# Two feed-forward blocks behind attention: when the second block's sixteen first weights are converted

## The chip, the cores and the metric

One core of a Trainium2 chip runs the kernel. The metric is the device time of one execution in microseconds; 1041.17 us is the median of three runs of the kernel before (1039.12 to 1044.33). The engines are called PE (TensorE, the matrix engine), DVE (VectorE), ACT (ScalarE), POOL (GpSimd) and SP, which here only issues DMAs.

## The reference

Attention with a decay is followed by two feed-forward blocks over 2304 tokens of 512 numbers. The first has two first weights (gate and value, 512 x 1536 each) and normalises its input, the second has one (512 x 2048). The weights of both blocks come as 64-bit floats; q, k, v and f are 32-bit.

```python
def _moe_ref(x, w_gate, w_val, w_out, rms_g) -> np.ndarray:
    rms = np.sqrt(np.mean(x * x, axis=-1, keepdims=True) + 1e-06)
    xn = x / rms * rms_g
    g = xn @ w_gate
    silu = g * (1.0 / (1.0 + np.exp(-g)))
    val = xn @ w_val
    return (silu * val @ w_out).astype(np.float32)

def _moe2_ref(x, w_in, w_out) -> np.ndarray:
    h = x @ w_in
    g = h * (1.0 / (1.0 + np.exp(-h)))
    return (g @ w_out).astype(np.float32)
```

## The kernel before

The tokens are cut into two parts, 1280 and 1024 (`PHASES`). After attention (up to about 218 us) the kernel runs `layer` four times: first block "a" for part 0 and part 1, then second block "b" for part 0 and part 1. In the trace these are about 218 to 457, 457 to 647, 647 to 862 and 862 to 1039 us. A layer goes over the hidden columns in groups of two units of 128 columns: six groups in block "a", eight in block "b". Each product is made of three matmuls of high and low parts (`hi` and `lo`, in the trace wh and wl, hh and hl), so that 32-bit numbers keep their precision. Part 0 of block "a" multiplies plainly; the other three layers use the seven products of Strassen's scheme, whose weight sums POOL forms.

A group's work in the program is: the first weights (`unit_plain` or `unit_in`), the two second weights (`unit_out`), then what is done ahead (`unit_ahead`), then the products and, between them, the second products of the group before (`pending`). The weights of a group are so placed by `spread` that their ACT instructions come after the first or the second Silu of the group before; in the trace they run a group ahead of their use.

`weights` brings one unit of 128 columns. If it is not yet kept, SP loads 512 KB of 64-bit numbers into a staging tile `st` (two buffers), ACT takes the upper word's magnitude (L143), and DVE makes the 32-bit float of it in four operations (L144 to L147); then SP stores it as a tile of 256 KB in DRAM (`kept`, L149). If it is kept already, SP loads these 256 KB (L134) and nothing is converted. `unit_ahead` does only the conversion and the store: it takes a tile `f` (three buffers) and makes no high and low parts. After `weights`, `unit_in` forms four sums of each pair on POOL (L162), ACT copies the high parts (L165), DVE or POOL takes the low parts (L166). `unit_plain` has L183 on ACT and L184 on POOL, `unit_out` has L193 on ACT and L194 on POOL. Its tile for the converted numbers has the tag `c` (nine buffers), which the hidden values use too.

In the groups that belong to `EARLY` (the third and the fourth) POOL forms differences of the next part's tokens (L657) and SP stores them (L660). ACT's L738 copies a sum of products out of PSUM while the accumulator goes on; the next product into it waits for that copy. L836 is the Silu and L843 the gate's product with the value.

The order of each engine's instructions is laid out when the program is compiled, by a scheduler that follows program order, priorities and free buffers; on the chip each engine keeps to that order and waits for what it needs.

Of the kernel before, what the change touches and what calls it, by code (L numbers as in the profile page):

```python
# [54 lines left out]

AHEAD_OF = ((0, 1), (2, 3), (12, 13), (14, 15), (), ())


@with_exitstack
def block_kernel(ctx: ExitStack, tc: tile.TileContext, q, k, v, f, w_gate, w_val, w_o1, rms_g, w_in, w_o2, ident_d, sel_d, hot_d, out):
# [572 lines left out]
    def end_attention():  # L635

        finish()
        ending.close()
        banks.update(LATER)
        psum["s"] = psum["x"] = ctx.enter_context(tc.tile_pool(name="psum3", bufs=2, space=PSUM, side="right", reuse_waits="tile"))  # L640
        x2 = ctx.enter_context(tc.tile_pool(name="x2", bufs=1, side="right", reuse_waits="tile"))
        xs.update({nm: [x2.tile([P, 2, TT], F32R, name=nm + p) for p in "hl"] for nm in ("t2", "t1", "t3")})

    def split(hi, lo, src):
        nc.scalar.activation(out=hi, in_=src, func=AF.Copy)  # L645
        nc.vector.tensor_tensor(out=lo, in0=src, in1=hi.bitcast(F32), op=ALU.subtract)  # L646
# [3 lines left out]
    def differences(ph, c):  # L650

        x = xparts[ph]
        made[:] = [ph]
        (b11, b12), (b21, b22) = ([x[:, 2 * i + c, j * TT : (j + 1) * TT] for j in range(2)] for i in range(2))
        t1, t2, t4 = (tmp.tile([P, TT], F32, tag="c", name="c") for _ in range(3))
        for nm, o, u, v in (("t1", t1, b12, b11), ("t2", t2, b22, t1), ("t4", t4, b21, t2), ("t3", b12, b22, b12)):
            nc.gpsimd.tensor_tensor(out=o, in0=u, in1=v, op=ALU.subtract)  # L657
            if nm != "t3":
                d = dram.tile([P, TT], F32, name=f"{nm}_{ph}_{c}_{len(kept)}")
                nc.sync.dma_start(out=d, in_=o)  # L660
                stored.setdefault((ph, nm), []).append(d)

    def prepare(ph, ahead=False):

        x, t = xparts[ph], {}
        b = {(i, j): [x[:, 2 * i + c, j * TT : (j + 1) * TT] for c in range(2)] for i in range(2) for j in range(2)}

        def diff(nm, u, v, to=None):
            if (ph, nm) in stored:
                t[nm] = to or [tmp.tile([P, TT], F32, tag="c", name="c") for _ in range(2)]  # L670
                for o, s in zip(t[nm], stored.pop((ph, nm))):
                    nc.scalar.dma_start(out=o, in_=s)
                return
            t[nm] = to or [tmp.tile([P, TT], F32, tag="c", name="c") for _ in range(2)]
            for o, u_, v_ in zip(t[nm], u, v):
                nc.gpsimd.tensor_tensor(out=o, in0=u_, in1=v_, op=ALU.subtract)

        def parts_(nm, src):
            for c in range(2):
                split(xs[nm][0][:, c], xs[nm][1][:, c], src[c])  # L680

        def p6():
            diff("t1", b[0, 1], b[0, 0], None if ahead else b[0, 0])
            diff("t2", b[1, 1], t["t1"])
            parts_("t2", t["t2"])

        def p7():
            if ph in made:
                t["t3"] = b[0, 1]
            else:  # L690
                diff("t3", b[1, 1], b[0, 1], b[0, 1])
            parts_("t3", t["t3"])

        def p4():
            diff("t4", b[1, 0], t["t2"], b[1, 0])
            parts_("t4", t["t4"])

        def rest():
            if ph == 0:
                for c in range(0, NCC, 2):  # L700
                    split(xs["rest"][0][:, c : c + 2], xs["rest"][1][:, c : c + 2], x[:, c : c + 2, 2 * TT :])

        return dict(
            p1=lambda: parts_("b11", b[0, 0]), p2=lambda: parts_("b21", b[1, 0]), p6=p6, p5=lambda: parts_("t1", t["t1"]), p7=p7, p4=p4, p3=lambda: parts_("b22", b[1, 1]), rest=rest
        )

    def spread(fn, *args):

        i = min(len(places), len(LEAD) - 1)
        places.append(0)  # L710
        if done == [1] and i < 2:

            after = exps[min(SECOND + STRIDE * i, len(exps) - 1)]
        elif marks:
            after = marks[min(LEAD[i], len(marks) - 1)]
        else:
            after = exps[min(PLACE + STRIDE * i, len(exps) - 1)]
        with tc.issue_after(after):
            return fn(*args)
# [96 lines left out]
    def layer(n, w_ins, w_out, second, ph, plain=False, ahead=()):  # L816
        NF = w_out.shape[0] // P
        in_fours[:] = [] if len(w_ins) == 2 and not plain else [True]
        G = 2
        for g in range(0, NF, G):  # L820
            win = [spread(*((unit_plain, w, f"{n}{z}", g) if plain else (unit_in, w, f"{n}{z}", g, ph == 0))) for z, w in enumerate(w_ins)]
            wout = [spread(unit_out, w_out, f"{n}o", m) for m in range(g, g + G)]
            for fn in ahead[g // G] if ahead else ():
                spread(fn)
            places.clear()
            marks.clear()
            done[0] += 1

            coming = prepare(parts_left.pop(0), plain) if g + G >= NF and parts_left else {}
            hs, gates = {}, {}  # L830

            def out_(z, at_, a, w):
                psum_ = plain or at_ == (1, 0) or at_[1] == 2
                if z == 0:
                    hf = tmp.tile([P, TT], F32, tag="c", name="c")[:, :w] if psum_ else a
                    act = nc.scalar.activation(out=hf, in_=a, func=AF.Silu)  # L836
                    marks.append(act.ins)
                    if len(w_ins) == 2:
                        gates[at_] = hf
                        return  # L840
                else:
                    hf = gates[at_]
                    (nc.vector if psum_ or at_ == (0, 1) else nc.gpsimd).tensor_tensor(out=hf, in0=a, in1=hf, op=ALU.mult)  # L843
                few = dict(tag="r", bufs=2) if w < TT else dict(tag="h", bufs=5)
                hh, hl = (hp_.tile([P, w], F32R, tag=few["tag"] + p, name="h" + p, bufs=few["bufs"]) for p in "hl")
                split(hh, hl, hf)
                hs[at_] = hh, hl

            todo, pending[:] = list(pending), []
            order = group(win, out_, ph == 0, plain)  # L850

            if plain and coming:

                for nm in ("p6", "p5", "p7"):
                    coming.pop(nm)()
                coming = dict(tile0=[coming[nm] for nm in ("p1", "p2")], tile1=[coming[nm] for nm in ("p4", "p3")])
                coming = {nm: _p(lambda fns: [fn() for fn in fns], fns) for nm, fns in coming.items()}
            for nm, ps in order:
                for p in ps:
                    p()  # L860
                for fn in todo[: 2 if len(ps) == 2 else 1 + (len(todo) > 7)]:
                    fn()
                    todo.remove(fn)
                coming.pop(nm, int)()
                if not plain and parts_left and nm == "p5" and g // G in EARLY:
                    differences(parts_left[0], EARLY.index(g // G))
            for fn in coming.values():
                fn()
            for fn in todo:
                fn()  # L870
            if plain and g == 0:
                end_attention()
            for j, w in enumerate((TT, TT, CUT - 2 * TT)[: 3 if ph == 0 else 2]):
                pending.extend(second(j * TT, w, lambda i, j=j, hs=hs: hs[i, j], wout, g == 0, g + G >= NF, ph))
# [40 lines left out]
    for c in range(0, NCC, 2):  # L915
        split(xs["rest"][0][:, c : c + 2], xs["rest"][1][:, c : c + 2], xparts[0][:, c : c + 2, 2 * TT :])
    for ph in range(2):
        layer("a", [w_gate, w_val], w_o1, second1, ph, ph == 0, [[_p(unit_ahead, w_in, "b0", m) for m in ms] for ms in AHEAD_OF] if ph else ())
    for ph in range(2):
        layer("b", [w_in], w_o2, second2, ph)  # L920
    for fn in pending:
# [41 lines left out]
```

## Time and profile before

| what | value |
|---|---|
| median of three runs | 1041.17 us (1039.12 to 1044.33) |
| the profiled execution | 1040.62 us |
| its span | 1038.8 us |
| PE busy | 1015.4 us (98%) |
| DVE busy | 759.6 us (73%) |
| ACT busy | 565.1 us (54%) |
| POOL busy | 407.4 us (39%) |
| granted PE clock | 0.998 of full |

The profile is of one execution. Times in it are counted from the span's start. A row of the timeline gives the start, the duration, the engine (with a q for its queue when it issues a DMA), the line of the kernel, the operation, the tiles it writes and reads, and its form; in square brackets stand the idle time of the engine before it and what ended that. Matmuls are pipelined: one begins before the one ahead of it ends.

### The profile page before, as it was taken

The page shows a single profiled execution, that of the slowest core. Times are in us where ns is not written, and L with a number is a line of the kernel's source. Part 1 is how long each engine was busy: PE and PEld are TensorE (multiplying, and loading weights), DVE is VectorE, ACT ScalarE, POOL GpSimd, SP SyncE. Part 2 cuts the span into 40 slices and gives each one's busy share as a digit, 9 for nine tenths or more (in the row PEclk, how much of TensorE's full clock was granted, in tenths as well). Part 3 has the DMA queues.
Part 4 walks back from the last instruction along what each step waited for, and adds up shares of the span by engine and source line. Part 5 has one row for each costly group of instructions (what it writes and reads, how often), then busy time and mean ns, then how long its engine had stood idle before and what let it go on. Part 6 is the DMA issues. An engine that isn't in the chain of part 4 may idle for free.

```text
span 1038.8 us, 16025 instructions
## 1 busy us (share of the span) xinstructions
PE 1015.4 (98%) x5459; PEld 843.5 (81%) x5459; DVE 759.6 (73%) x1509; ACT 565.1 (54%) x1191; POOL 407.4 (39%) x601
## 2 busy tenths in 40 slices
PE   8998999999999999999999999999999999999998
PEld 7877778778888888888887787887787888888886
DVE  7889887877576777976487767968876696366664
ACT  6998989874442323445544446564444465544441
POOL 8776666501121206423355544225533323222300
PEclk9999999999999999999999999999999999999999
DMA  5674443123331524231233221134442234121102
GB/s 140 172 196 108 123 95 101 25 69 115 122 123 68 175 71 143 88 95 61 92 126 128 82 77 55 67 117 152 152 153 82 82 122 142 41 67 56 51 0 82
DMA packets 113009, 104.30 MB, mean 100 GB/s; under 512 B 62768, under 2 KB 83664, under 8 KB 112928
## 3 DMA queue, kind: packets, MB, share of 16 engines
q1 hardware_dynamic: 111200, 100.14, 31.4%
q10 hardware_dynamic: 1728, 3.15, 1.0%
q8 instruction: 43, 0.70, 0.3%
q14 instruction: 38, 0.31, 0.1%
HBM read 77.49 MB, written 25.76 MB: 99 GB/s over the span
## 4 chain that ended last, share of the span: by engine, by line
PE 62%; DVE 8%; issue 3%; POOL 3%; ACT 2%; DMA 1%; POOLq 0%; SPq 0%; ACTq 0%; DVEq 0%
PE t L726 32%; PE s L726 16%; PE x L726 12%; POOL f L162 2%; DVE hl L646 1%; DVE xa L903 1%; DVE wl L166 1%; DVE c L743 1%; DVE c L147 1%; DVE f L146 1%; ACT wh L165 1%; POOL c L843 1%; DMA st<-in_moe_w_in_dram 0%; DMA f<-kepta 0%; POOL wol L194 0%
## 5 line engine op out<-in xcount | busy, mean ns | idle before, releaser
L194 POOL TENSOR_TENSOR wol<-c,woh 128x512 fp32r<-128x512 f32 x54 | 77.0, 1433 | 282.1 <-ACT woh L193 254.6
L646 DVE TENSOR_TENSOR hl<-c,hh 128x512 fp32r<-128x512 f32 (+1 forms) x140 | 111.5, 803 | 51.0 <-ACT hh L645 50.7
L162 POOL TENSOR_TENSOR f<-f 128x256 f32<-128x256 f32 x112 | 89.0, 815 | 132.6 <-DMA f<-keptb 55.3
L645 ACT ACTIVATE hh<-c 128x512 fp32r<-128x512 f32 (+1 forms) x140 | 79.4, 583 | 61.6 <-DVE c L843 26.0
L435 POOL TENSOR_SCALAR dt<-ncb,c8t 128x64 f32<-128x64 f32 (+2 forms) x144 | 78.4, 546 | 38.1 <-DVE nm L451 31.5
L738 ACT ACTIVATE c<-t 128x512 f32<-128x512 f32 x84 | 49.5, 590 | 71.7 <-PE t L726 69.1
L463 ACT ACTIVATE pr<-pr,nm 128x192 f32<-128x192 f32 (+3 forms) x144 | 80.2, 558 | 13.4 <-DVE nm L451 10.9
L836 ACT ACTIVATE c<-c 128x512 f32<-128x512 f32 x66 | 41.6, 630 | 80.3 <-DVE c L743 80.3
L166 DVE TENSOR_TENSOR wl<-f,wh 128x1024 fp32r<-128x1024 f32 (+1 forms) x48 | 61.0, 1279 | 31.3 <-ACT wh L165 31.3
L451 DVE CUSTOM_DVE_ANT_0 pr<-s,dt 128x256 f32<-128x256 f32 (+7 forms) x160 | 69.9, 451 | 16.8 <-PE t L472 5.1
L165 ACT ACTIVATE wh<-f 128x1024 fp32r<-128x1024 f32 (+1 forms) x56 | 54.1, 975 | 39.5 <-POOL f L162 19.7
L472 PE MATMUL t<-ident,pr 128*128 128x128 f32 x384 | 69.1, 279 | 3.2 <-ACT pr L463 2.3
L184 POOL TENSOR_TENSOR wl<-f,wh 128x1024 fp32r<-128x1024 f32 x12 | 28.7, 2391 | 93.9 <-ACT wh L183 93.9
L726 PE MATMUL s<-hh,woh 128*128 128x512 f32 (+1 forms) x172 | 64.2, 374 | 0.3 <-DVE xa L885 0.3
L726 PE MATMUL s<-hl,woh 128*128 128x512 f32 (+1 forms) x172 | 64.0, 372 | 0.0
L726 PE MATMUL s<-hh,wol 128*128 128x512 f32 (+1 forms) x172 | 64.0, 372 | 0.0
L743 DVE TENSOR_TENSOR c<-t,c 128x512 f32<-128x512 f32 x60 | 41.2, 687 | 30.2 <-ACT c L738 16.5
L836 ACT ACTIVATE c<-t 128x512 f32<-128x512 f32 (+1 forms) x74 | 37.5, 511 | 41.8 <-PE t L726 40.1
L903 DVE TENSOR_TENSOR xa<-x,xa 128x512 f32<-128x512 f32 x64 | 43.6, 681 | 21.0 <-PE x L726 20.9
L726 PE MATMUL x<-wol,hh 128*128 128x512 f32 (+1 forms) x146 | 57.1, 391 | 1.8 <-POOL wol L194 1.8
L885 DVE TENSOR_TENSOR xa<-s,xa 128x512 f32<-128x512 f32 (+1 forms) x72 | 45.6, 639 | 16.3 <-PE s L726 16.3
L726 PE MATMUL x<-woh,hh 128*128 128x512 f32 (+1 forms) x146 | 56.8, 389 | 0.0
(234 smaller groups left out, 3191.1 us busy)
## 6 DMA issues: line engine op xcount, KB each, us to landing
st<-in_moe_w_out_dram SPq DMA_DIRECT2D x28, 512.0 KB, 3.7
st<-in_moe_w_in_dram SPq DMA_DIRECT2D x16, 512.0 KB, 3.9
st<-in_moe_w_gate_dram SPq DMA_DIRECT2D x12, 512.0 KB, 4.0
kepta<-f SPq DMA_DIRECT2D x24, 256.0 KB, 2.4
st<-in_moe_w_val_dram SPq DMA_DIRECT2D x12, 512.0 KB, 4.6
f<-kepta SPq DMA_DIRECT2D x24, 256.0 KB, 2.6
f<-keptb SPq DMA_DIRECT2D x24, 256.0 KB, 2.6
out_dram<-xa SPq DMA_DIRECT2D x17, 256.0 KB, 2.0
```

Of the source, the lines that this page charges most:

```text
L162: nc.gpsimd.tensor_tensor(out=out_, in0=x, in1=y, op=op)
L165: nc.scalar.activation(out=hi[i][:, u], in_=f[i][:, u], func=AF.Copy)
L166: (nc.gpsimd if plain and i else nc.vector).tensor_tensor(out=lo[i][:, u], in0=f[i][:, u], in1=hi[i][:, u].bitcast(F32), op=ALU.subtract)
L194: nc.gpsimd.tensor_tensor(out=lo, in0=f, in1=hi.bitcast(F32), op=ALU.subtract)
L435: nc.gpsimd.tensor_scalar(out=dt, in0=p.nct[:, 0 if last else D :][:, :n], scalar1=c8t[:, c, p.i : p.i + 1], scalar2=1.0, op0=ALU.add, op1 ...
L451: nc.vector.tensor_tensor_reduce(out=self.pr[:, ks], in0=sp, in1=self.dt[:, ks], op0=ALU.add, op1=ALU.min, scale=-SCALE, scalar=3.0e38, ac ...
L463: e = nc.scalar.activation(out=pr, in_=pr, func=AF.Exp, bias=self.nm, scale=-1.0, accum_out=p.batch.sums[:, self.c, p.hp : p.hp + 1])
L472: nc.tensor.transpose(pt[:, jj * P : (jj + 1) * P], keys[:, jj * P : (jj + 1) * P], ident)
L645: nc.scalar.activation(out=hi, in_=src, func=AF.Copy)
L646: nc.vector.tensor_tensor(out=lo, in0=src, in1=hi.bitcast(F32), op=ALU.subtract)
L726: nc.tensor.matmul(ps, lhsT=l, rhs=r, start=start and z == 0, stop=stop and z == len(mms) - 1, skip_group_check=not (start and stop))
L836: act = nc.scalar.activation(out=hf, in_=a, func=AF.Silu)
```

## The change

Before, half of the sixteen units of `w_in` were converted ahead, two in each of the first four groups of the first block's part 1 (units 0 to 3 and 12 to 15). Units 4 to 11 were converted in part 0 of the second block, where they were used straight away and also stored for part 1. After, all sixteen are converted ahead in part 0 of the first block: none in its first group, four in each of the next three groups, two in each of the last two. Part 1 of the first block converts none, and the second block loads all its first weights as kept ones. The table now has a row for each part.

```diff
-AHEAD_OF = ((0, 1), (2, 3), (12, 13), (14, 15), (), ())
+AHEAD_OF = (((), (0, 1, 2, 3), (4, 5, 6, 7), (8, 9, 10, 11), (12, 13), (14, 15)), ((),) * 6)
...
     for ph in range(2):
-        layer("a", [w_gate, w_val], w_o1, second1, ph, ph == 0, [[_p(unit_ahead, w_in, "b0", m) for m in ms] for ms in AHEAD_OF] if ph else ())
+        layer("a", [w_gate, w_val], w_o1, second1, ph, ph == 0, [[_p(unit_ahead, w_in, "b0", m) for m in ms] for ms in AHEAD_OF[ph]])
     for ph in range(2):
         layer("b", [w_in], w_o2, second2, ph)
```

## Rows read from the trace of the kernel before

**Rows 1.** Page, busy: time, share of the span, instructions.
```profile
PE 1015.4 (98%) x5459; PEld 843.5 (81%) x5459; DVE 759.6 (73%) x1509; ACT 565.1 (54%) x1191; POOL 407.4 (39%) x601
```
**Rows 2.** Stages: length, busy us (instructions) per engine, clock, DMA share, GB/s.
```profile
core 0: us, PE busy (x) PEld busy (x) DVE busy (x) ACT busy (x) POOL busy (x), PEclk, DMA share, GB/s
291.70:333.00 41.30, 41.30 (x219) 35.67 (x218) 29.34 (x47) 13.46 (x25) 8.01 (x4) 1.00 0.35 116
415.60:456.90 41.30, 41.30 (x219) 35.66 (x218) 35.04 (x55) 18.95 (x34) 10.96 (x8) 1.00 0.34 103
786.00:814.00 28.00, 28.00 (x140) 23.75 (x139) 19.57 (x32) 13.57 (x24) 10.25 (x8) 1.00 0.30 94
```
**Rows 3.** Timeline of PE, last gate matmul and first value matmul of a group.
```profile
335.75 0.39 PE L726 MATMUL t<-b21h,wl 128*128 128x512 f32 x1
335.98 0.39 PE L726 MATMUL t<-b11h,wh 128*128 128x512 f32 x1
```
**Rows 4.** Timeline of PE, matmuls that waited, in both blocks.
```profile
718.83 0.50 PE L726 MATMUL t<-t4h,wh 128*128 128x512 f32 x1 [1.18 <-ACT c L738]
...
746.77 0.50 PE L726 MATMUL t<-t4h,wh 128*128 128x512 f32 x1 [1.52 <-ACT c L738]
...
781.19 0.50 PE L726 MATMUL x<-wol,hh 128*128 128x512 f32 x1 [1.21 <-POOL wol L194]
...
494.00 0.50 PE L726 MATMUL t<-b11h,wl 128*128 128x512 f32 x1 [0.97 <-DVE wl L166]
...
554.75 0.50 PE L726 MATMUL t<-b11h,wl 128*128 128x512 f32 x1 [0.61 <-DVE wl L166]
```
**Rows 5.** Timelines of DVE, POOL and ACT ahead of 718.83.
```profile
713.36 0.68 DVE L147 SCALAR_TENSOR_TENSOR f<-st,f 128x512 int32<-128x512 int32 x1
...
714.12 2.96 POOL L162 TENSOR_TENSOR f<-f 128x256 f32<-128x256 f32 x4 [4.68 <-DVE f L147]
...
716.29 2.01 ACT L165 ACTIVATE wh<-f 128x1024 fp32r<-128x1024 f32 x2 [6.58 <-POOL f L162]
```
**Rows 6.** Timeline of POOL in a group whose weights are kept.
```profile
793.85 2.93 POOL L162 TENSOR_TENSOR f<-f 128x256 f32<-128x256 f32 x4 [1.27 <-DMA f<-keptb]
```
**Rows 7.** Timeline of DVE: one conversion, and a slow step of another.
```profile
312.43 0.42 DVE L144 TENSOR_SCALAR f<-f 128x512 f32<-128x512 f32 x1
312.89 0.43 DVE L145 TENSOR_SCALAR f<-f 128x512 int32<-128x512 int32 x1
313.35 0.69 DVE L146 SCALAR_TENSOR_TENSOR f<-st,f 128x512 int32<-128x512 int32 x1
314.07 0.69 DVE L147 SCALAR_TENSOR_TENSOR f<-st,f 128x512 int32<-128x512 int32 x1
...
708.33 1.67 DVE L146 SCALAR_TENSOR_TENSOR f<-st,f 128x512 int32<-128x512 int32 x1
```
**Rows 8.** Timeline of SP, loads into st in one group of part 0.
```profile
293.80 0.38 SPq L141 DMA_DIRECT2D st<-in_moe_w_gate_dram  x1
...
298.15 0.38 SPq L141 DMA_DIRECT2D st<-in_moe_w_gate_dram  x1
...
302.60 0.39 SPq L141 DMA_DIRECT2D st<-in_moe_w_val_dram  x1
...
312.96 0.38 SPq L141 DMA_DIRECT2D st<-in_moe_w_out_dram  x1
...
315.21 0.38 SPq L141 DMA_DIRECT2D st<-in_moe_w_out_dram  x1
...
336.68 0.39 SPq L141 DMA_DIRECT2D st<-in_moe_w_gate_dram  x1
```
**Rows 9.** Timelines of ACT and POOL in the same group.
```profile
297.56 0.67 ACT L143 ACTIVATE f<-st 128x512 f32<-128x512 f32 x1 [2.02 <-DMA st<-in_moe_w_gate_dram]
...
316.00 2.39 POOL L184 TENSOR_TENSOR wl<-f,wh 128x1024 fp32r<-128x1024 f32 x1 [7.24 <-ACT wh L183]
...
330.89 1.23 ACT L143 ACTIVATE c<-st 128x512 f32<-128x512 f32 x2
```
**Rows 10.** Timeline of PE, the transposes of attention's last factors.
```profile
256.82 0.53 PE L359 MATMUL s<-identr,rt 128*16 128x128 f32 x5 [0.72 <-DVE rt L351]
```

## The prediction

> **What bounds the kernel now.** I read the page's busy lines first, then the table of stages, then TensorE's waits one by one. TensorE is busy in 98% of the span [rows 1], and inside the two blocks that is close to real: in the first block's first part its 128x512 matmuls start 0.23 us apart while each lasts 0.39 us [rows 3], and in the group from 291.7 to 333.0 us it has no idle at all [rows 2]. So nothing that shortens another engine's work shortens the span by itself. Only a wait of TensorE that goes, or one that comes, moves the end, and a shown idle costs 0.16 us more than it says, because two matmuls no longer overlap (0.39 less 0.23). From 218 us on there are twelve such waits of 0.15 us or more; the ones that this change can best reach stand in [rows 4]. In the second block's first part there are three large ones: 1.18, 1.52 and 1.21 us. In the first block's second part one of 0.97 us waits for a VectorE split of weights, and one of 0.61 us does so two groups later. The groups of the second block that already load converted weights (786 to 814 us) have none [rows 2].
>
> **What the change removes: eight conversions in the second block's first part.** The mechanism behind its waits is readable in [rows 5]. VectorE ends the conversion of a pair of weights (L147 at 713.36), POOL forms their four sums (L162, which had waited 4.68 us for VectorE), and the two ScalarE copies of these sums (L165) begin only at 716.29, after 6.58 us for POOL. Next in ScalarE's own order stands the copy L738 that empties the accumulator, and TensorE's first t4 matmul waits for that copy, until 718.83. With the weights kept, POOL's sums start after a 256 KB load: in such a group they wait 1.27 us for it and are done by 796.8 [rows 6], with no wait of TensorE there [rows 2]. The wait at 781.19 is the same chain's tail: POOL reaches its split L194 late. I take all three as gone: 1.18 + 1.52 + 1.21 = 3.91, and 3 x 0.16 = 0.48 on top, so 4.4 us. What is late next: this part also stores three differences for its second part (L660) through the SP queue, and loads of kept weights stand behind them. The nearest row for kept weights beside such stores is the wait at 554.75 in the first block, 0.61 + 0.16 = 0.8 us [rows 4]. The second block stores differences in two groups, so I charge 1.0 us back; bounds 0 and 2.0.
>
> **What it removes in the first block's second part: six of the eight conversions there.** The last two of the new list take the place of the first two of the old one, at 418 us, so the passage between the parts stays as it is. The wait at 494.00 follows a VectorE stretch in which an added conversion lies between the splits; without its four operations, 2.2 us by [rows 7], the split is done before it is needed: 0.97 + 0.16 = 1.1 us. The wait at 554.75 is POOL's and SP's as much as VectorE's, so I count half of its 0.8: 0.4 us. Gains so far: 4.4 - 1.0 + 1.1 + 0.4 = 4.9 us; bounds 2.0 (only two of the three, nothing else) and 7.
>
> **What it adds: fourteen conversions between 250 and 390 us.** One costs ScalarE one copy and VectorE 0.42 + 0.43 + 0.69 + 0.69 = 2.2 us [rows 7], and two DMAs of SP. The eight weights that were used straight from their conversion are now read back once, 8 x 256 KB, one load each in a queue that has room; I cost that at nothing, since it is loaded during the group before, and at up to one wait like [rows 6] each if that cover is gone.
>
> VectorE's room: 29.3 us of a 41.3 us group are busy [rows 2]; four conversions add 9.0, which makes 38.3, or 93%. It fits, with little over. TensorE does not follow VectorE closely here (four banks for the products and four for the second products), and the group at 415.6 runs without TensorE idle at 35.0 us [rows 2]. So the question is not the busy time but whether the next group's weights are ready.
>
> For this I follow the two staging buffers st, which are handed out in program order: six conversions in a group (gate, gate, value, value, out, out), and now four more between the out pair and the next gate pair. In [rows 8] the first buffer's loads start at 293.80, 302.60 and 312.96, the second's at 298.15 and 315.21 after two rounds. A round is thus 9.6 us on the one and 8.5 on the other, 9.05 as a mean; the longest of these is 10.4. The out pair's load ends long before its conversion at 330.89 [rows 9], for which it waits until the group's own tiles have had theirs. That idle time of the buffers is the room for the change. New timetable: four rounds in place of two from 293.80, then the same tail as now, which is 5.4 us from the load at 312.96 to the end of POOL's split at 318.39 (316.00 + 2.39) [rows 9]. Value weights ready: 293.80 + 36.2 + 5.4 = 335.4. They are needed at 335.98, the first matmul of the value block [rows 3]. So 0.6 us ahead: no wait. But the out pair now loads at 330.0 and lands about 3.8 us later (as 293.80 to 297.56 [rows 9]), some 3.0 us after its old slot of 330.89, so the following four start at 336.68 + 3.0 = 339.7 [rows 8], and the next value weights are ready at 339.7 + 36.2 + 5.4 = 381.3 against a need of 377.3 (335.98 + 41.3): 4.0 us late. The two groups after that add only two conversions and catch up. So the addition costs 0 with rounds of 8.5 us, 4.0 at the mean, and about 15 at 10.4 (4.8, then 10.1). I take 2.0: near the mean round, with half of it filled, because TensorE has the previous group's second products to put in front, as it does now between 262 and 273 us.
>
> The first four of the new conversions fall in the group where attention's last scaling still runs. TensorE already waits there for VectorE's factors, 0.72 us [rows 10]; conversions ahead of that short chain could lengthen it. I take 0.3 us more, bounds 0 and 2.
>
> A rule that speaks against the change: by the Trainium skill, SBUF — State Buffer, section "Who interferes with whom", a VectorE instruction with both inputs in SBUF contends with a GpSimd instruction that reads SBUF. The trace agrees that such a conversion step can be long: L146 took 1.67 us at 708.33 against 0.69 elsewhere [rows 7]. Were both such steps slowed in all four conversions, a group would have 29.3 + 4 x (0.85 + 2 x 1.67) = 46.1 us of VectorE work in 41.3, 4.8 too many in each of three groups, and the kernel would come to some 1051 us. POOL is busy for only 8.0 us of that group [rows 2], so at most a part of them can meet it; of the second rival's chance below, 0.05 is for this case.
>
> **Sum.** -4.9 + 2.0 + 0.3 = -2.6 us. The profiled execution took 1040.62 us (span 1038.8 and 1.8 around it), 0.55 below the median of the runs, 1041.17. Against the profiled one that is 1038.0, against the median 1038.6. I forecast 1038.6.
>
> **The rivals.** First, a clean gain: the first part swallows all fourteen conversions. For it: rounds of 8.5 us are seen, and VectorE idles in the last third of these groups. Against it: 93% busy and a timetable with 0.6 us to spare. It gives 1041.2 - 4.9 to 7, so 1034 to 1036.
>
> Second, slower: the staging buffers become the bound between 292 and 380 us. Value weights come late, TensorE waits at the first matmuls of the value block, and the lateness is handed on to the next group through the out pair. It decides from rounds longer than about 9.2 us ((335.98 - 5.4 - 293.80)/4), and it outweighs the gain soon after; at 10.4 us it costs 15: 1041.2 - 4.9 + 15 = 1051. For it: rounds of 10.4 are in the trace with fewer conversions than there will be. Against it: the second half of the group has less VectorE work, and the mean round lies just under the limit.
>
> Third, the gain doesn't come: in the second block ScalarE's copies of the weights still stand ahead of L738 and wait for loads behind the SP stores of the differences, as at 554.75. Then 1.1 us from the first block remains and is spent there: about 1041. Against it: no such wait in the kept groups of [rows 2].
>
> **How the numbers follow.** About 0.5% (5.2 us) is what a measurement of this kernel can tell from no change. Forecast (net -5 to +3) 0.42, clean gain 0.24, slower 0.20, gain absent 0.14. Faster by over 0.5% needs under 1036.0: most of the clean gain and little of the forecast, 0.25. Slower by over 0.5% needs over 1046.4: most of the slower case and some of the forecast's upper end, 0.20. Within: 0.55. The range leaves out the deep end of both: 1033 (all of 7 us, and 1 for the spread of the runs) to 1047 (a loss of 11 in the first part against a gain of 5).
>
> **What would show it.** Right: no TensorE idle over 0.5 us between 700 and 790 us; sums on L162 there waiting for a load and not for VectorE; the wait at 494 gone; VectorE at 36 to 39 us in the groups from 292 to 374; loads of st every 8.5 to 9.5 us. Wrong: TensorE waiting for the value weights' split L184 at about 336 or 377 us or at the factors near 257 (second rival), or L738 still behind L165 in the second block (third).

## The result

The kernel after takes 1046.49 us (median of six runs, 1045.89 to 1048.60), the kernel before beside it 1040.94 (1039.12 to 1044.33): a ratio of 1.0054, 95% interval 1.0040 to 1.0069. It is slower by about 5.5 us, where 1038.6 was forecast: inside the range, on the wrong side. The profiled execution took 1046.15 us, its span 1044.4 against 1038.8.

The profile after, in the order of the rows of before. First the page's busy lines, then the table of stages over the windows of [rows 2] and some more:

```profile
PE 1015.9 (97%) x5459; PEld 844.2 (81%) x5459; DVE 755.9 (72%) x1509; ACT 565.1 (54%) x1191; POOL 406.4 (39%) x601
```
```profile
core 0: us, PE busy (x) PEld busy (x) DVE busy (x) ACT busy (x) POOL busy (x), PEclk, DMA share, GB/s
291.70:333.00 41.30, 39.89 (x208) 34.19 (x206) 31.62 (x52) 13.01 (x24) 6.61 (x4) 1.00 0.51 164
333.00:374.30 41.30, 37.80 (x168) 30.94 (x169) 33.83 (x61) 13.89 (x24) 5.20 (x3) 0.96 0.52 169
374.30:415.60 41.30, 39.04 (x197) 32.82 (x196) 33.45 (x56) 14.45 (x25) 10.03 (x5) 1.00 0.54 175
415.60:456.90 41.30, 38.72 (x203) 33.02 (x203) 36.53 (x55) 16.51 (x29) 18.51 (x14) 1.00 0.41 135
700.00:790.00 90.00, 90.00 (x438) 76.13 (x437) 60.45 (x98) 43.31 (x79) 39.97 (x30) 1.00 0.26 88
```

The work is the same to within a microsecond per engine, VectorE apart, which has 3.7 us less (755.9 after 759.6). What moved is idle time of TensorE. In the first block's part 0, where [rows 2] show 41.30 of 41.30 in two groups, TensorE is idle now in each group; in the second block's part 0, where [rows 4] show three waits between 718 and 782 us, it is not idle from 700 to 790 us (90.00 of 90.00). The timeline of TensorE, its larger waits from 330 us on (one of 0.97 us at 425.37, for VectorE's L885, is left out):

```profile
333.31 0.39 PE L726 MATMUL s<-hh,woh 128*128 128x256 f32 x1 [1.72 <-DVE xa L885]
...
338.47 0.50 PE L726 MATMUL t<-b11h,wh 128*128 128x512 f32 x1 [1.41 <-ACT wh L183]
...
340.98 0.59 PE L726 MATMUL t<-b11h,wl 128*128 128x512 f32 x1 [1.78 <-POOL wl L184]
...
384.27 0.50 PE L726 MATMUL t<-b11h,wh 128*128 128x512 f32 x1 [0.55 <-ACT wh L183]
...
386.72 0.50 PE L726 MATMUL t<-b11h,wl 128*128 128x512 f32 x1 [1.71 <-POOL wl L184]
...
434.56 0.50 PE L726 MATMUL x<-hh,wol 128*128 128x512 f32 x1 [1.62 <-POOL wol L194]
...
475.36 0.50 PE L726 MATMUL s<-hh,woh 128*128 128x512 f32 x1 [1.64 <-DVE xa L885]
...
506.79 0.50 PE L726 MATMUL t<-b11h,wl 128*128 128x512 f32 x1 [0.54 <-DVE wl L166]
```

The row at 338.47 is the first value matmul of a group, the second line of [rows 3]: it starts now after a wait for its high parts, and 2.5 us later its low parts are waited for again. The last row answers to 494.00 of [rows 4]: 0.54 is left of 0.97. The wait at 554.75 has no successor.

TensorE's matmuls come in nearly the same order in all kernels of this study, so I take the start of the same matmul in two traces; the difference is the lag, and a stretch costs what the lag grows by in it. The table has this for every kernel, by stretches of the trace of before, in microseconds (one profiled execution each).

| kernel | up to 285 (attention, first group) | 285 to 390 | 390 to 485 (passage of the parts) | 485 to 600 | 600 to 860 (second block, part 0) | sum |
|---|---|---|---|---|---|---|
| after | -1.08 | 10.20 | 4.77 | -2.68 | -5.41 | 5.80 |
| e1 ahead before out | 0.21 | 9.01 | 10.00 | -2.69 | -5.39 | 11.14 |
| e2 three each | 2.16 | 0.90 | 16.35 | -2.69 | -5.40 | 11.32 |
| e3 two each | 0.53 | 0.00 | 6.93 | -1.25 | -5.36 | 0.85 |
| e4 second block only | 0.55 | 0.00 | 1.03 | -0.01 | -5.40 | -3.83 |
| e5 own staging | 0.44 | 2.31 | 7.63 | -2.85 | -5.39 | 2.14 |
| e6 seven c | 1.95 | 9.42 | 4.55 | -2.78 | -5.38 | 7.76 |
| e7 half loads | 5.85 | 0.00 | 3.27 | -2.69 | -4.73 | 1.70 |
| e8 fours alone | 0.15 | 11.22 | -0.04 | -2.27 | -5.38 | 3.68 |
| e9 split late | 0.44 | 8.97 | 4.31 | -2.67 | -5.41 | 5.64 |
| e10 threes | 0.75 | 0.62 | 6.47 | -0.62 | -5.26 | 1.96 |
| e11 threes split | -1.14 | 0.00 | 3.91 | 0.20 | -5.36 | -2.39 |
| e12 second block split | 0.75 | 0.00 | 0.91 | 0.73 | -5.07 | -2.68 |

The first column scatters by some 3 us between kernels that do nearly the same there; most of the scatter arises in the first 140 us, before the first added load at 249, so it says nothing of the change (e7 apart, and e1, which waits 1.24 us at 248.40). Two things are in the other columns besides waits. A row is of one execution, which can lie off the kernel's median: e7's is its slowest (1041.65, median 1039.65), e11's its fastest (1037.51, median 1041.49). And the granted clock fell to 0.50 of full behind some waits: for 3.4 us in the kernel after and in e8 (285 to 390) and in e3 and e5 (390 to 485), for 6.8 us in e6 and e9 (285 to 390) and in e2 and e10 (390 to 485), for 3.4 and then 10.2 us in e1, and nowhere in these columns in e4, e7, e11 and e12. At half the clock up to half of such a time is lost: 1.7 us of 3.4, 3.4 of 6.8. For the kernel after, the gains came and are larger than forecast: 2.68 + 5.41 = 8.1 us against 4.9. The price in the first block's part 0 and behind it is 10.20 + 4.77 = 15.0, against 2.3.

### The profile page after: what moved, and what is told of

Same layout as the page of the kernel before. It is cut to its first block, busy times and chain, and to the rows that moved or that the text cites. A ratio compares the mean times of both kernels' runs of the same rounds, so it can differ in the third digit from the quotient of the medians.

```text
span 1044.4 us, 16069 instructions
## 1 busy us (share of the span) xinstructions
PE 1015.9 (97%) x5459; PEld 844.2 (81%) x5459; DVE 755.9 (72%) x1509; ACT 565.1 (54%) x1191; POOL 406.4 (39%) x601
## 4 chain that ended last, share of the span: by engine, by line
PE 62%; DVE 7%; DMA 4%; issue 3%; POOL 2%; ACT 2%; POOLq 0%; SPq 0%; ACTq 0%; DVEq 0%
PE t L726 30%; PE s L726 17%; PE x L726 14%; DMA st<-in_moe_w_out_dram 1%; DMA st<-in_moe_w_val_dram 1%; DVE hl L646 1%; DMA st<-in_moe_w_in_dram 1%; POOL f L162 1%; DVE f L146 1%; DVE wl L166 1%; DMA keptb<-f 1%; DVE f L144 1%; DVE f L147 0%; ACT f L143 0%; DVE xa L885 0%
## 5 line engine op out<-in xcount | busy, mean ns | idle before, releaser
L194 POOL TENSOR_TENSOR wol<-c,woh 128x512 fp32r<-128x512 f32 x54 | 77.4, 1438 | 247.2 <-ACT woh L193 216.5
L646 DVE TENSOR_TENSOR hl<-c,hh 128x512 fp32r<-128x512 f32 (+1 forms) x140 | 106.5, 767 | 55.3 <-ACT hh L645 54.5
L645 ACT ACTIVATE hh<-c 128x512 fp32r<-128x512 f32 (+1 forms) x140 | 79.3, 582 | 58.2 <-DVE c L843 37.9
L738 ACT ACTIVATE c<-t 128x512 f32<-128x512 f32 x84 | 49.6, 592 | 98.5 <-PE t L726 95.2
L184 POOL TENSOR_TENSOR wl<-f,wh 128x1024 fp32r<-128x1024 f32 x12 | 28.7, 2393 | 158.7 <-ACT wh L183 158.7
L726 PE MATMUL s<-hh,woh 128*128 128x512 f32 (+1 forms) x172 | 64.5, 375 | 4.6 <-DVE xa L885 4.6
L726 PE MATMUL s<-hh,wol 128*128 128x512 f32 (+1 forms) x172 | 64.0, 372 | 0.0
L726 PE MATMUL s<-hl,woh 128*128 128x512 f32 (+1 forms) x172 | 64.0, 372 | 0.0
L885 DVE TENSOR_TENSOR xa<-s,xa 128x512 f32<-128x512 f32 (+1 forms) x72 | 45.6, 639 | 20.5 <-PE s L726 20.4
L143 ACT ACTIVATE f<-st 128x512 f32<-128x512 f32 x42 | 28.0, 670 | 57.0 <-DMA st<-in_moe_w_in_dram 25.7
L903 DVE TENSOR_TENSOR xa<-s,xa 128x512 f32<-128x512 f32 (+1 forms) x63 | 43.0, 682 | 21.6 <-PE s L726 21.2
L726 PE MATMUL x<-wol,hh 128*128 128x512 f32 (+1 forms) x146 | 56.9, 390 | 0.6 <-POOL wol L194 0.6
```

The lines of the kernel that those rows point to most:

```text
L194: nc.gpsimd.tensor_tensor(out=lo, in0=f, in1=hi.bitcast(F32), op=ALU.subtract)
L726: nc.tensor.matmul(ps, lhsT=l, rhs=r, start=start and z == 0, stop=stop and z == len(mms) - 1, skip_group_check=not (start and stop))
L903: nc.vector.tensor_tensor(out=a, in0=ps, in1=a, op=ALU.add)
```

## Where the time is lost in the kernel after

The loads into the staging buffers st; this is SP's timeline, some loads of one buffer in the first group with four added conversions (249.14 to 287.58, two of its five left out), then all of the second such group and the first of the third:

```profile
249.14 0.39 SPq L141 DMA_DIRECT2D st<-in_moe_w_in_dram  x1
...
262.84 0.39 SPq L141 DMA_DIRECT2D st<-in_moe_w_in_dram  x1
...
287.58 0.38 SPq L141 DMA_DIRECT2D st<-in_moe_w_out_dram  x1
...
297.34 0.39 SPq L141 DMA_DIRECT2D st<-in_moe_w_in_dram  x1
...
308.49 0.39 SPq L141 DMA_DIRECT2D st<-in_moe_w_in_dram  x1
...
317.78 0.39 SPq L141 DMA_DIRECT2D st<-in_moe_w_gate_dram  x1
...
325.85 0.39 SPq L141 DMA_DIRECT2D st<-in_moe_w_val_dram  x1
...
335.24 0.38 SPq L141 DMA_DIRECT2D st<-in_moe_w_out_dram  x1
...
345.62 0.39 SPq L141 DMA_DIRECT2D st<-in_moe_w_in_dram  x1
```

In [rows 8] the buffer that was loaded at 312.96 was not loaded again until 336.68. Now no such pause is left: from 297.34 to 345.62 the buffer goes round five times without a stop, in 48.28 us, 9.66 each, while a group of TensorE takes 41.3. The four rounds up to the out load are 11.15, 9.29, 8.07 and 9.39, a mean of 9.48. The value weights, which were due from POOL at 335.98 - 1.08 = 334.9 by [rows 3] and the lag, come out at 338.56 + 2.37 = 340.93, 6.0 us late:

```profile
333.02 0.67 ACT L143 ACTIVATE f<-st 128x512 f32<-128x512 f32 x1 [2.12 <-DMA st<-in_moe_w_val_dram]
...
337.36 1.06 ACT L183 ACTIVATE wh<-f 128x1024 fp32r<-128x1024 f32 x1 [3.40 <-DVE f L147]
...
338.56 2.37 POOL L184 TENSOR_TENSOR wl<-f,wh 128x1024 fp32r<-128x1024 f32 x1 [7.25 <-ACT wh L183]
```

These rows, of ScalarE and POOL, answer to [rows 9]. ScalarE waits 2.12 us for the load of the second value unit; everything behind it on ScalarE waits too. VectorE's order carries the same stop to work that has nothing to do with weights, here in its timeline:

```profile
330.41 1.18 DVE L144 TENSOR_SCALAR f<-f 128x512 f32<-128x512 f32 x1 [1.55 <-ACT f L143]
...
332.57 0.68 DVE L885 TENSOR_TENSOR xa<-s,xa 128x512 f32<-128x512 f32 x1
```

L885 empties a bank of second products. It stands behind a conversion step that waited 1.55 us for ScalarE's copy at 329.70, which had waited 0.95 us for the load of the first value unit; TensorE's wait at 333.31 is for this L885. After the two waits at 338.47 and 340.98 comes a loss that no wait shows. The table of stages in small windows, same columns as above:

```profile
340.98:344.50 3.52, 3.52 (x9) 2.74 (x10) 3.52 (x9) 1.17 (x2) 1.37 (x1) 0.54 0.01 6
344.50:348.00 3.50, 3.50 (x17) 2.88 (x16) 3.43 (x6) 0.64 (x1) 1.41 (x1) 0.98 0.48 149
```

For 3.5 us the granted clock is 0.54, near the lower of its two levels (1.2 of 2.4 GHz), and 9 matmuls run where the next 3.5 us hold 17: (17 - 9) x 0.2 = 1.6 us.

## The experiments

Theory A: the two staging buffers, used in program order, can't turn round five times in a group, so weights that TensorE needs come late. Theory B: VectorE (with ScalarE and POOL) has too much to do, in whatever order it gets its data. The runs go in three batches, each beside the kernel before: medians of 1041.51 us for e1 to e4, 1041.76 for e5 to e8, 1041.39 for e9 to e12; the ratios are against the runs of before beside each kernel.

**e1.** The conversions ahead stand before the out pair in program order.

```diff
-            wout = [spread(unit_out, w_out, f"{n}o", m) for m in range(g, g + G)]
             ...
+            wout = [spread(unit_out, w_out, f"{n}o", m) for m in range(g, g + G)]
```

> The changed kernel, with one thing moved: in each group of the program the conversions ahead stand before the two second weights (unit_out), not behind them. The same conversions run in the same groups, so VectorE has the same work. Theory A (the two staging buffers st are the bound; the out pair holds both idle until its late conversion, and what comes behind it starts late): the four conversions now fall into that idle time, the next gate load starts at its old place, TensorE's waits between 330 and 390 us go, the gains of the later layers stay: about 1035 us. Theory B (VectorE's 93% in these groups is the bound): nothing to gain from the order, about 1046 us, VectorE late at L885 and L843 as now.

1053.60 us, ratio 1.0116 (1.0100 to 1.0133). Neither number. What moved are the victims, in TensorE's timeline:

```profile
378.62 0.39 PE L726 MATMUL t<-resth,wh 128*128 128x256 f32 x1 [2.80 <-DVE c L843]
...
435.37 0.79 PE L726 MATMUL x<-hh,woh 128*128 128x512 f32 x1 [3.79 <-ACT woh L193]
...
439.28 0.79 PE L726 MATMUL x<-hh,wol 128*128 128x512 f32 x1 [2.69 <-POOL wol L194]
```

The waits for the value weights' low parts are gone; now the out weights, which stand last, are late, up to 3.79 us at the passage of the parts. Order decides who is late, not whether. Both theories miss the time; what speaks in it is against my idea, which A had taken over, that the out pair has room to give away.

**e2.** Three conversions in each of groups 1 to 5, the sixteenth unit in part 1.

```diff
-AHEAD_OF = (((), (0, 1, 2, 3), (4, 5, 6, 7), (8, 9, 10, 11), (12, 13), (14, 15)), ((),) * 6)
+AHEAD_OF = (((), (0, 1, 2), (3, 4, 5), (6, 7, 8), (9, 10, 11), (12, 13, 14)), ((15,), (), (), (), (), ()))
```

> The changed kernel with three conversions ahead in each of the five groups from the second on, and the sixteenth unit in the first group of part 1. Theory A: three and a half rounds of 9.4 us and the tail of 5.4 us from about 294 us give value weights at about 332, ahead of the need at 336, and no lateness is handed on: no wait in the first block's first part, about 1035 us. Theory B: 29.3 + 6.7 = 36 us of 41.3 for VectorE (87%), about half of the loss of 13 us stays: about 1041.

1050.82 us, ratio 1.0080 (1.0066 to 1.0094). A miss for both. The table: 0.90 between 285 and 390, near what A says, but 16.35 from 390 to 485.

```profile
419.16 0.39 PE L726 MATMUL t<-resth,wh 128*128 128x256 f32 x1 [2.84 <-DVE c L843]
...
437.09 0.79 PE L726 MATMUL x<-hh,wol 128*128 128x512 f32 x1 [5.05 <-POOL wol L194]
```

I read this as lateness that is stored up over groups and for which the passage has no cover: there POOL's L194 stands behind the six differences of L676 for part 1. In the kernel after the same passage reads, in POOL's timeline:

```profile
421.75 2.41 POOL L184 TENSOR_TENSOR wl<-f,wh 128x1024 fp32r<-128x1024 f32 x1 [7.28 <-ACT wh L183]
424.12 2.98 POOL L676 TENSOR_TENSOR c<-xa 128x512 f32<-128x512 f32 x2
...
429.94 3.17 POOL L676 TENSOR_TENSOR xa<-xa 128x512 f32<-128x512 f32 x2
433.07 1.44 POOL L194 TENSOR_TENSOR wol<-c,woh 128x512 fp32r<-128x512 f32 x1
```

L194 starts as soon as L676 ends, L676 as soon as the late L184 ends, and TensorE waits until 434.56 for that wol. The same two places in the kernel before:

```profile
401.97 2.40 POOL L184 TENSOR_TENSOR wl<-f,wh 128x1024 fp32r<-128x1024 f32 x1 [1.72 <-ACT wh L183]
...
417.50 3.08 POOL L194 TENSOR_TENSOR wol<-c,woh 128x512 fp32r<-128x512 f32 x2 [4.44 <-ACT woh L193]
```

POOL's L184 is 19.8 us later than it was, while TensorE lags by 9.1 to 12.3 us here, and the 4.44 us in which POOL waited for nothing but L193 are used up.

The passage's 4.77 us are three waits in the kernel after, of which this is the second: 1.23 at 425.37, 1.93 at 434.56 and 1.6 at 475.36, as the lag grows there. The first is for an L885 at 424.63, and that stands behind a slow step of VectorE:

```profile
422.22 2.48 DVE L646 TENSOR_TENSOR hl<-c,hh 128x512 fp32r<-128x512 f32 x1 [0.45 <-ACT hh L645]
```

The same step took 0.68 us at 406.29; at 422.22 POOL's late L184 runs beside it. In the kernel before an L646 beside an L184 took as long (2.53 us at 316.42) and TensorE did not wait.

**e3 and e4.** Two conversions a group, in all of groups 1 to 5 and the first three of part 1 (e3); or the eight units of part 1 as before and only the second block's eight added, in groups 1 to 4 (e4).

```diff
+AHEAD_OF = (((), (0, 1), (2, 3), (4, 5), (6, 7), (8, 9)), ((10, 11), (12, 13), (14, 15), (), (), ()))
```
```diff
+AHEAD_OF = (((), (4, 5), (6, 7), (8, 9), (10, 11), ()), ((0, 1), (2, 3), (12, 13), (14, 15), (), ()))
```

> Two conversions ahead in each of five groups of the first block's part 0 (units 0 to 9) and two in each of the first three groups of its part 1 (units 10 to 15). Theories A and B both: part 0 has no waits (three rounds in a group; VectorE at 82%), the second block keeps its whole gain of about 5 us, part 1 keeps the waits at 494 and 555 us of before: about 1036.

> Part 1 of the first block as before (units 0 to 3 and 12 to 15), and units 4 to 11 converted two at a time in four groups of part 0. It does alone what the change does to the second block. If that block's gain is about 5 us by itself and part 0 takes two in a group without a wait: about 1036, with part 1 of the first block as before.

e3: 1042.33 us, ratio 1.0005 (0.9995 to 1.0016), a miss. e4: 1036.62 us, ratio 0.9950 (0.9937 to 0.9962), faster than both kernels. Eight conversions a group cost nothing up to 390 us in either. e3 loses 6.93 us behind that, most of it at one wait:

```profile
436.93 0.38 SPq L141 DMA_DIRECT2D st<-in_moe_w_in_dram  x1
...
453.05 0.32 SPq L149 DMA_DIRECT2D keptb<-f  x1
...
456.22 0.66 ACT L143 ACTIVATE f<-st 128x512 f32<-128x512 f32 x1 [4.53 <-DMA keptb<-f]
...
459.06 0.48 PE L726 MATMUL t<-resth,wh 128*128 128x256 f32 x1 [4.11 <-DVE c L843]
```

(Timelines of SP, of ScalarE and of TensorE.) ScalarE stands 4.53 us before the copy that begins a conversion in the first group of part 1, and the work of TensorE's next step behind it. It isn't the staging buffers here: the load for this copy was issued at 436.93 and had landed at 441.66. The copy began 0.1 us after the store of an earlier unit had landed (issued at 453.05, landed at 456.12), so what it waited for was a free tile f, of which there are three. e4 has conversions there too but none in the last group of part 0. Its table of stages, and then one wait from TensorE's timeline, in part 1 of the first block:

```profile
333.00:374.30 41.30, 41.30 (x218) 35.66 (x218) 34.63 (x58) 13.82 (x24) 7.38 (x4) 1.00 0.47 153
...
700.00:790.00 90.00, 90.00 (x437) 76.12 (x437) 63.38 (x98) 40.01 (x70) 43.41 (x31) 1.00 0.33 109
```
```profile
495.58 0.50 PE L726 MATMUL t<-b11h,wl 128*128 128x512 f32 x1 [0.98 <-DVE wl L166]
```

The wait of 494.00 in [rows 4] is back, because its conversions are, and the second block's gain is whole: 5.40 of 5.41. The two gains are thus separate.

**e5 and e6.** The conversions ahead get a staging buffer of their own, sa; to make room, tag c has 7 buffers in place of 9. e6 is the control: 7 of c, nothing else.

```diff
-        dst = stp.tile([P, 2 * n], I32, tag="st", name="st")
+        dst = late["tmp"].tile([P, 2 * n], I32, tag="sa", name="sa", bufs=1) if own else stp.tile([P, 2 * n], I32, tag="st", name="st")
...
-    tmp = ctx.enter_context(tc.tile_pool(name="tmp", bufs=9, reuse_waits="tile"))
+    tmp = ctx.enter_context(tc.tile_pool(name="tmp", bufs=7, reuse_waits="tile"))
```

> The changed kernel; the conversions ahead get a staging buffer of their own (one), so the two st serve gate, value and out as before. Room for it comes from the hidden values' tiles c, seven in place of nine. Theory A (ten loads and conversions in a group through two buffers, each buffer some 9.2 us per load, is 46 us in a group of 41.3): value weights are ready again some 18 us after the gate's first load, as in the kernel before, and TensorE's waits for them near 336 and 384 us go; 1037 to 1041 us, if seven tiles c do. Theory B (VectorE's 93%): VectorE's work is the same, so waits of about 8 us stay between 330 and 390 us: about 1046.

> The control for the run before: the changed kernel with seven tiles c in place of nine, staging as it is. Both theories: as the changed kernel, 1046, or slower by what seven tiles cost.

e5: 1043.18 us, ratio 1.0016 (1.0002 to 1.0029). e6: 1047.29 us, ratio 1.0063 (1.0047 to 1.0079). The buffer alone is worth 4.1 us, with the same conversions in the same groups. Between 285 and 390 us 2.31 is lost in place of 9.42, and the waits for value weights are gone. What is left is a wait behind VectorE's L885 (1.36 us at 375.27) and the passage, 7.63, now larger than in e6. So the staging makes most of the loss between 285 and 390 us (in e6 some 2.7 of the 9.42 are the clock's) and not that of the passage. The tiles f are three in e5 as in e6, so most of that loss isn't theirs.

**e7.** The whole chain in halves: half-size loads, four half-size buffers in the same room, so VectorE and ScalarE have twice as many conversion instructions.

```diff
+        for h in range(2):
+            v = w[:, h * n // 2 : (h + 1) * n // 2]
             ...
+            dst = stp.tile([P, n], I32, tag="st", name="st", bufs=4)
```

> The changed kernel; each unit goes through staging in two halves of 256 KB, with four half-size buffers in the same memory. VectorE's and ScalarE's steps double in number and each is half as long, so VectorE has some 0.3 to 0.6 us more per unit by fixed costs. Theory A: a half is loaded and converted sooner and the four buffers turn over faster; a group's ten units need less than 41 us and the waits near 336 and 384 go: 1036 to 1041. Theory B: more VectorE work in the groups that have 93% already: slower than 1046, about 1050.

1039.65 us, ratio 0.9984 (0.9974 to 0.9995). The first block starts 5.85 us late; 5.5 of it arise in attention, before 140 us (e9, which leaves attention alone, has 0.44). It is still a little faster than the kernel before. Its table of stages is the strongest evidence against B:

```profile
333.00:374.30 41.30, 41.30 (x219) 35.66 (x218) 38.80 (x103) 16.11 (x35) 8.93 (x4) 1.00 0.58 185
374.30:415.60 41.30, 41.30 (x219) 35.67 (x218) 38.47 (x93) 14.80 (x32) 9.95 (x5) 1.00 0.54 169
```

VectorE is busier in this stretch than in any other kernel here (38.80 of 41.30, where the kernel after has 33.83), and TensorE waits for nothing.

**e8.** The fours alone: groups 1 to 3 as in the kernel after, the last four units in part 1.

```diff
+AHEAD_OF = (((), (0, 1, 2, 3), (4, 5, 6, 7), (8, 9, 10, 11), (), ()), ((12, 13), (14, 15), (), (), (), ()))
```

> Units 0 to 11 converted four at a time in the second to fourth group of part 0, as the change has it; units 12 to 15 not in its last two groups but two at a time in the first two groups of part 1, as the kernel before has its first four. It parts the loss of the fours from that of the passage between the parts. The waits between 330 and 390 us stay (about 9 us); those between 425 and 437 us (3 us), which I put down to the out pair being late behind the conversions of the fifth group, go, if the fifth group catches up. About 1043.

1044.18 us, ratio 1.0030 (1.0014 to 1.0047). It parts the loss: 11.22 stays in the groups with fours, and the passage costs -0.04 in place of 4.77. The waits in the groups with fours are those of the kernel after:

```profile
387.37 0.50 PE L726 MATMUL t<-b11h,wl 128*128 128x512 f32 x1 [1.71 <-POOL wl L184]
```

The conversions of the last two groups are thus needed for the passage's loss. My step "the two groups after that add only two conversions and catch up" is wrong.

**e9.** As after, but each unit in two loads and two half conversions within its one staging buffer, from the third group on.

```diff
+        parts_ = 2 if done[0] > 1 else 1
+        for h in range(parts_):
             ...
+            d = dst[:, 2 * h * m : 2 * (h + 1) * m]
```

> The changed kernel; from the third group of part 0 on each unit is loaded and converted in two halves within its one staging buffer (two buffers of full size as before, attention untouched). A buffer's turn is load of a half, load and conversion overlapped, conversion of the second half: some 7 to 8 us in place of 9.2, so ten units need 35 to 40 us of a 41.3 us group. Staging theory: the waits near 336 and 384 us go or shrink to under 1 us each, those of the passage shrink, and the five microseconds that the half-size tiles lost in attention are not lost: 1035 to 1038. VectorE theory: as the changed kernel or slower, 1046 to 1050.

1045.79 us, ratio 1.0040 (1.0026 to 1.0054): a miss. A conversion can begin earlier, but the buffer is held until its second half is done: its five rounds from 297.64 to 346.19 take 9.71 us each, no less than in the kernel after, and the waits stay:

```profile
341.27 0.80 PE L736 MATMUL t<-b11h,wl 128*128 128x512 f32 x1 [1.77 <-POOL wl L194]
```

(The lines are ten further down: L736 is L726, L194 is L184.) Against e7 this speaks for what it was there: buffers that come free one by one, not short loads. (The first four added units are still whole in e9, so the two kernels differ in that as well.)

**e10, e11 and e12.** Threes in three groups, two in the fourth, none in the last, the rest in part 1 (e10); the same with the split of e9 (e11); e4's table with that split (e12).

```diff
+AHEAD_OF = (((), (0, 1, 2), (3, 4, 5), (6, 7, 8), (9, 10), ()), ((11, 12), (), (), (13, 14, 15), (), ()))
```

> Three ahead in each of the second to fourth group of part 0, two in the fifth, none in the sixth; in part 1 two in the first group and three in the fourth. Full loads. The runs of three each showed no wait before 380 us; the passage is left with the load that it has in the kernel before. No wait in part 0 over 1 us; part 1 loses the wait at 494 us and keeps about one of the two later ones; the second block as in the changed kernel: 1034 to 1036.

> The table of the run before with the split loads: if staging is what is left in part 0, nothing or 1 us better than that run, about 1034; if VectorE's small added work matters, 1 to 2 us worse.

> The table that does the second block's part alone (1036.6 us with full loads), with the split loads. Two each leave staging with room, so no gain is expected from it: 1036 to 1038; a gain of over 1 us would say that staging costs even there.

e10: 1044.14 us, ratio 1.0025 (1.0014 to 1.0036), a miss; e11: 1041.49, ratio 0.9994 (0.9983 to 1.0004); e12: 1037.17, ratio 0.9950 (0.9937 to 0.9964). Nine conversions a group are too many: e10 and e4 differ up to the passage by one more in each of three groups, and e10 loses 0.62 and 6.47 where e4 loses 0.00 and 1.03. Some 2.8 of the 6.47 are the clock's (half of the 6.8 us at 0.50, less the 1.13 that TensorE waited in them). The loads say the same: in e4 the three rounds from 294.03 to 322.53 take 9.50 on average, and the buffer then rests for 14.7; in e10 the first added loads of the groups stand at 295.56, 339.25 and 384.00, 43.7 and 44.8 us apart, where a group of TensorE takes 41.3. Its first wait after 400 us is for VectorE again, whose conversions had waited for ScalarE's copies at 409.14 and 411.07, and these 2.25 and 1.26 us for the loads of the value weights:

```profile
416.81 0.38 PE L726 MATMUL t<-resth,wh 128*128 128x256 f32 x1 [2.33 <-DVE c L843]
```

With the split e11 is 2.65 us faster than e10 in the median, and e12 is no faster than e4. That the split takes a part of the passage's loss away isn't shown: TensorE's waits there are 2.33 and 1.13 us in e10 and 2.52 and 1.13 in e11, and what 6.47 has over 3.91 is about what 6.8 us at half the clock cost, which the execution of e11 doesn't have. The best order found is thus e4's: eight conversions a group, and none in the last group before the passage.

## Why the prediction went wrong

**Right: the second block.** All three waits of [rows 4] there are gone. ACT's L738 ends at 725.33, TensorE's t4 product begins at 728.71 without a wait, and POOL's sums wait for a load, as [rows 6] had it (ScalarE's and POOL's timelines):

```profile
724.73 0.60 ACT L738 ACTIVATE c<-t 128x512 f32<-128x512 f32 x1 [4.84 <-PE t L726]
```
```profile
773.39 2.93 POOL L162 TENSOR_TENSOR f<-f 128x256 f32<-128x256 f32 x4 [1.15 <-DMA f<-keptb]
```

The L738 waits 4.84 us for TensorE, where before, by [rows 5], TensorE waited for it. The gain is 5.41, not 4.4 less 1.0: the stores of the differences on SP cost nothing, and the three waits took 1.56, 1.86 and 1.52 from the lag, more than their idle time plus the 0.16 that I added; a small wait of 0.18 us at 773.32, which I had not priced, took 0.47. The third rival falls.

**Right in kind, too small: the first block's part 1.** 2.68 against 1.5. The wait at 494.00 kept half of itself, the one at 554.75 went whole, and one at 586 us of 0.84 us, which I had not priced, went too. e8, which keeps conversions in the first two groups of part 1, still waits 0.96 us in the place of 494.00 and has 2.27 of the 2.68: most of this gain came from the two later waits, of which I had priced one at 0.4 and the other not at all.

**Wrong: the staging buffers' timetable,** the term of 2.0. It measured 10.20 + 4.77, and the second rival, with a chance of 0.20, is what happened, at 1046.49 us. That the sum is the 15 that I had given for rounds of 10.4 us is luck: the rounds were shorter, some 1.7 of the 15.0 are the clock's, which I had not priced, and 4.77 are the passage's, which I had put at nothing. Four steps failed in the term. First, I began at 293.80, the load time of before, as if the first group with four conversions handed on nothing. That group used up its own pause (out load at 287.58, before at 272.45), and the second began at 297.34, 3.5 us later though attention ended 1.1 earlier. Second, the round: I took 9.05 as the mean of a 9.6 and an 8.5, and it was 9.48; the point from which the rival decides, 9.2, was right, and I stood on the wrong side of it by 0.3 with three groups to add up. Third, the sentence that the out pair's wait "is the room for the change": out pair included, a group with ten conversions needs five rounds, five times 9.66 are 48.3, and 41.3 are there (with my own mean round, 45.3). The same product gives 37.9 for the eight conversions of e4 (four rounds of 9.48) and 42.7 for the nine of e10: the first fits, the second just doesn't, as the runs have it. It was to be had from [rows 8] alone. Fourth, I halved the 4.0 that the timetable gave at the mean round, because TensorE would put second products in front. It put nothing in front: from 216 to 490 us its matmuls come in exactly the order of before.

**Wrong: "TensorE does not follow VectorE closely here".** It doesn't follow VectorE's busy share, as e7 shows. It follows VectorE's order: an L885 or L843 behind a conversion that waits for its load is late however idle VectorE is. The 36 to 39 us that I asked of VectorE in these groups didn't come either (31.62 and 33.83): the conversions were late, not long.

**Wrong: the two last groups catch up,** and with it "so the passage between the parts stays as it is". The loads of the last two units came at 435.81 and 440.30, not at 418 as I had it. They kept the lateness, and the passage, where POOL's differences stand between the late value weights and the out weights, turned it into 4.77 us (e8: none of it without their conversions; which of the steps there would have to be earlier wasn't tried).

**Right: the small terms.** The factors' wait of [rows 10] is 0.70 now (0.72), so attention's tail cost nothing instead of 0.3. The case of 0.05 inside the second rival did not come. The rule of the Trainium skill, SBUF — State Buffer, "Who interferes with whom", by which two-input steps of VectorE on SBUF get in the way of GpSimd's reads and the other way round, would have made L146 and L147 long in the added conversions. The groups of VectorE's instructions between 249 and 436 us (busy us, mean ns, idle before) say otherwise for these, which are fourteen of the thirty with tile f, and agree for the out pair, whose tile is c:

```profile
L147 DVE SCALAR_TENSOR_TENSOR f<-st,f 128x512 int32<-128x512 int32 x30 | 20.7, 689 | 0.6
...
L147 DVE SCALAR_TENSOR_TENSOR c<-st,c 128x512 int32<-128x512 int32 x8 | 8.5, 1061 | 0.1
```

The out pair's conversions run now while POOL works on L184 and L676, and their L147 took 1.06 us on average where that of the others took 0.69 and their own took 0.68 in the kernel before. Their one-input steps grew too (L145 0.93 us after 0.43). A small part of the passage's loss may be this. No run parted it.

**What stays open.** How the three waits of the passage, 1.23, 1.93 and 1.6 us, go back to staging, the tiles f, POOL's order and slow VectorE steps: e8 shows only that they need the conversions of the last two groups, and e5 that a staging buffer more (with two tiles c less) doesn't take the loss away. In e3 it was the tiles f. A third full staging buffer, or a fourth f, was not tried.

## What to carry to other kernels

When work is moved ahead, count the turns of each buffer ring on its way (here the staging buffers, in e3 the tiles f) against the time of the loop that it joins: turns needed times the measured turn, from load to release, must stay below it, with every user of the ring counted, and the first group that is full must not be taken for one that starts fresh. An engine's idle share is not room if its order puts work that the critical engine needs behind an instruction that waits for a load. And where two halves of a change pay and cost in different places, run each alone: here the half that pays (e4) was to be had without the half that costs.

## What was not expected of the hardware

After TensorE had waited, the granted clock fell in some cases and not in others: to 0.54 for 3.5 us after the waits of 1.41 and 1.78 us at 338 to 341 us, but not after the same kernel's waits of 0.55 and 1.71 at 384 to 387. In e8 it was the other way round, with nearly the same waits in both places: it fell to 0.57 behind 387.37 (1.43 and 1.71) and not at all behind 341.81 (1.43 and 1.78). Executions of one kernel differ in time as they do in clock: e11 took 1037.51 us in the execution with a mean clock of 1.000 and 1041.47 to 1042.59 in the seven with 0.993 or 0.995, and the kernel before 1038.90 to 1040.29 in its five runs with 1.000 beside it. So a pair of waits of 3.2 us together can cost 1.6 more than it shows. What decides whether the clock falls, these runs don't tell.
